# Attention and GEGLU layers on one core: the emitter orders TensorE by a timed event model, with exponentials without a bias operand, a compact out-projection and a two-phase start of layer 2

## The chip, the cores and the metric

The kernel runs on one core of a Trainium2 chip. The metric is device time in microseconds (us) of one execution; lower is better. Every program was run several times, always beside runs of the kernel before on the same chip.

## The reference

Two identical layers, each an attention block and a GEGLU block with residuals. 2048 tokens, width 512, 32 heads of 16, FFN width 1792, all in bfloat16.

```python
def _A_ref(x, wqkv, wo):                       # attention
    q, k, v = split_heads(x @ wqkv)            # 32 heads of 16
    p = softmax((q @ k.T) * 16 ** -0.5)        # 2048 x 2048 for each head
    return merge_heads(p @ v) @ wo

def _B_ref(x, w_gate, w_up, w_down):
    return (gelu_tanh(x @ w_gate) * (x @ w_up)) @ w_down

for _ in range(2):
    x = x + _A_ref(layernorm(x), wqkv, wo)
    x = x + _B_ref(layernorm(x), w_gate, w_up, w_down)
```

## The kernel before

The work of a layer is 32 *units*: 4 blocks of 512 queries times 8 groups of 4 heads. A unit has 64 score tiles (128 keys x 512 queries), made in 22 *slots* of two or three tiles, each slot in one of two sets of three PSUM banks (PSUM is the memory that the matmuls write into). In a slot ScalarE takes the exponential of two or three tiles in one ACTIVATE. In 16 of the 22 slots the third tile goes to VectorE instead, which makes a piecewise approximation of the exponential in int16 (tile `fPI`, then three shifted copies `fPP`). TensorE multiplies all of these with V (17 columns: 16 of V and a column of ones, which gives the row sums) into one accumulator bank. After a query block's 8 units come its out-projection, layer norm and FFN, the *post* of the block, as side work among the units of the next block.

The kernel is written by a small emitter: every operation is appended to its engine's list with the tiles it reads and writes, and semaphores are derived from that. Each engine runs its list in order. So if TensorE's next operation waits, every later one on TensorE waits with it, ready or not. The order comes from counters of steps and "tokens", not from times:

```python
def mm512(pairs, rkeys, evac, cols=512):       # a projection: 4 or 8 matmuls into bank 6
    b = misc.next()
    ...
    pe(fn, rkeys, [BK[b]])
    evac(b)                                    # VectorE reads the bank, at once in the list
    return 216.0 * n + 100

while nxt < len(seqs) or unit_order:           # one slot for each step
    ...
    if state["gslots"] is not None: emit_gslots()   # 7 gelu slots in a row
    a_slot(layer, u, tiles, ds)                # 3 score matmuls, exponential
    if shifts: do_shift()
    if step % 2 or not posts: run_pv(step)     # weighted sums of slots at least LAG = 2 old
    flush_norm(step)
    tokens = min(CAP, tokens + RATE)
    if step % 2 == 0:
        ...                                    # projections and posts while tokens last
```

A post waits for the normalised tile by counting steps (`yield from delay(12)`), then puts its out-projection into TensorE's list. The exponential has its bias as a column in memory:

```python
sch.op("act", lambda e: e.activation(PT[...], PS[:, b0:b0 + na, :], ACTF.Exp,
                                     bias=EBIAS[:, 0:1], scale=1.0 / (OCT * LOG2E)), ...)
```

The out-projection uses a padded layout: a head group's 16 real rows in each 32, so 8 matmuls of which half the rows are zero. The reciprocals of the row sums go through DRAM and come back into one buffer (`NRB = 1`):

```python
for i, g in enumerate(gs):                     # 4 head groups at a time
    for j in range(4):
        dma("sp", ..., RB[32 * j:32 * j + 16, slot, :], src, ...)
    sch.op("pool", ... AT[:, g, :] = OS[:, os_, :] * RB[:, slot, :])
def out_proj(qb, qt):
    return mm512([(AT[:, g, qt * 128:(qt + 1) * 128], WOP[:, g, :]) for g in range(NG)], ...)  # NG = 8
```

Of the kernel before, what the change touches and what calls it, by code (L numbers as in the profile page):

```python
# [14 lines left out]
AP = bass.AP  # L15
# [5 lines left out]
class _Op:  # L21
    __slots__ = ("eng", "idx", "fn", "deps", "waits", "sig", "val", "grp", "vc", "marks")

    def __init__(self, eng, idx, fn, grp=None):
        self.eng = eng
        self.idx = idx
        self.fn = fn
        self.deps = {}
        self.waits = []
        self.sig = False  # L30
        self.val = 0
        self.grp = grp
        self.vc = None
        self.marks = ()


class _Sched:
    SELF_ORDERED = ("pe",)

    def __init__(self):  # L40
        self.streams = {}
        self.track = {}
        self.last_w = {}
        self.last_r = {}
        self.order = []
        self.groups = {}
        self.alias = {}

# [13 lines left out]
    def add_engine(self, name):  # L62
        self.streams[name] = []
        self.track[name] = []

# [4 lines left out]
    def op(self, eng, fn, r=(), w=(), grp=None):  # L70
# [35 lines left out]
        self.order.append(o)  # L106
        return o
# [46 lines left out]
def _emit_fast(nc, es, x_in, wqkv, wo, wg, wu, wd, out, n_rep=2):  # L154
# [22 lines left out]
    NPH = 4  # L177
    OCT = 1024.0
    LOG2E = 1.4426950408889634
    QSCALE = OCT * LOG2E * DH ** -0.5  # L180
    SHIFT = 3.0
    LOG2_4M = 2.0566325
    L_LO, L_HI = 32.0, 1e30
# [13 lines left out]
    WOP = sb("fWOP", [128, NG, D], BF)  # L197
    NWR = 5
# [5 lines left out]
    EBIAS = sb("fEBIAS", [128, 1], F32)  # L204
# [4 lines left out]
    NPS = 4  # L209
    PP = sb("fPP", [128, NPS, 2048], I16)  # L210
    NQS = 4
    Q = sb("fQ", [128, NQS, 512], BF)
    NOS = HB + 2
    OS = sb("fOS", [128, NOS, 512], F32)
    LT = sb("fLT", [128, 128], F32)
    NRB = 1
    RB = sb("fRB", [128, NRB, 512], F32)
    AT = sb("fAT", [128, NG, 512], BF)
# [23 lines left out]
    class Ring:  # L242
        def __init__(self, banks):
            self.banks = list(banks)
            self.pos = 0

        def next(self):
            self.pos += 1
            return self.banks[self.pos % len(self.banks)]

    misc = Ring([MISC])

    def dma(eng, grp, dst, src, r=(), w=(), serial=False):
        if grp not in sch.groups:
            sch.add_dma_group(grp, serial=serial)
        sch.op(eng, lambda e: e.dma_start(dst, src), r=r, w=w, grp=grp)  # L256

    def pe(fn, r, w):
        sch.op("pe", fn, r=r, w=w)
# [3 lines left out]
    for t in range(4):  # L263
        dma("pool", "ldx0_%d" % t, X[:, t, :], x_in[0, 128 * t:128 * (t + 1), :], w=[("X", t)])
    for b in range(1, NQB):
        dma("pool", "ldx%d" % b, X[:, 4 * b:4 * b + 4, :],
            x_in[0, 512 * b:512 * (b + 1), :].rearrange("(a p) c -> p a c", p=128),
            w=[("X", 4 * b + i) for i in range(4)])
    dma("sp", "ldw_k", WK[:], wq_src[:, :, D:2 * D], w=[("WK",)])
    dma("sp", "ldw_q", WQ[:], wq_src[:, :, 0:D], w=[("WQ",)])  # L270
    dma("sp", "ldw_v", WV[:], wq_src[:, :, 2 * D:3 * D], w=[("WV",)])
# [7 lines left out]
    for j in range(4):  # L279
# [3 lines left out]
    sch.op("pool", lambda e: e.memset(EBIAS[:], -SHIFT / LOG2E), w=[("EBIAS",)])  # L283
    sch.op("dve", lambda e: e.memset(PS[:, ACC, :], 0.0), w=[BK[ACC]])
    sch.op("pool", lambda e: e.memzero(WOP[:].rearrange("p a b -> p (a b)")),
           w=[("WOP", j, p) for j in range(4) for p in range(2)])
    for j in range(4):
        for p in range(2):
            src = AP(wo.tensor, wo.offset + (32 * j + 16 * p) * D, [[D, 16], [128 * D, NCK], [1, D]])
            dst = AP(WOP, 32 * j * NG * D + p * D, [[NG * D, 16], [2 * D, NCK], [1, D]])  # L290
            dma("sp", "ldw_o%d%d" % (j, p), dst, src, w=[("WOP", j, p)])
    sch.op("pool", lambda e: e.memset(AP(VP, 16, [[NKT * H * VW, 128], [VW, NKT * H]]), 1.0), w=[("VPONE",)])
    sch.op("pool", lambda e: e.memset(RB[:], 0.0), w=[("RB", i, j) for i in range(NRB) for j in range(4)])
    sch.op("pool", lambda e: e.memset(OKL[:], 1.0), w=[("OKL",)])
    sch.op("pool", lambda e: e.memset(OKV[:], 1.0), w=[("OKV",)])
    sch.op("pool", lambda e: e.memset(LT[:], 1.0), w=[("LT", i, j) for i in range(HB) for j in range(4)])
# [13 lines left out]
    def wload():  # L310
# [12 lines left out]
        dma("sp", "wr%d" % s, dst, src, w=[("WR", s)], serial=True)  # L323
# [11 lines left out]

    def xn(i, alt):
        return AT[:, i, :] if alt else HT[:, i, :]

    def xnkey(i, alt):
        return ("AT", i) if alt else ("HT", i)  # L340

    def ln_tiles(tts, check=False, alt=False):
        n = len(tts)
        for i, tt in enumerate(tts):
            sch.op("dve", lambda e, i=i, tt=tt: e.bn_stats(ST[:, i, :], X[:, tt, :]), r=[("X", tt)], w=[("ST", i)])  # L345
            sch.op("dve", lambda e, i=i: e.bn_aggr(MV[:, i, :], ST[:, i, :]), r=[("ST", i)], w=[("MV", i)])
# [3 lines left out]
        sch.op("pool", lambda e: e.tensor_scalar(LNS[:, 0, 0:n], var, LN_EPS, None, op0=ALU.add), r=mvk, w=[("LNS",)])  # L350
        sch.op("pool", lambda e: e.tensor_tensor(LNS[:, 1, 0:n], LNS[:, 0, 0:n], CM05[:, 0:n], op=ALU.pow),
               r=[("LNS",), ("CM05",)], w=[("LNS",)])
        sch.op("pool", lambda e: e.tensor_scalar(LNS[:, 2, 0:n], mean, -1.0, None, op0=ALU.mult),
               r=mvk + [("LNS",)], w=[("LNS",)])
        for i, tt in enumerate(tts):
            sch.op("pool", lambda e, i=i, tt=tt: e.tensor_scalar(  # L356
                xn(i, alt)[:, 0:D], X[:, tt, :], LNS[:, 2, i:i + 1], LNS[:, 1, i:i + 1], op0=ALU.add, op1=ALU.mult),
                r=[("X", tt), ("LNS",)], w=[xnkey(i, alt)])
        if check:
            sch.op("dve", lambda e: e.scalar_tensor_tensor(OKV[:, 0:n], var, L_HI, OKV[:, 0:n],  # L360
                                                           op0=ALU.is_le, op1=ALU.mult),
                   r=mvk + [("OKV",)], w=[("OKV",)])

    def transpose_tile(i, tt, alt=False, eng="dve"):
        b = misc.next()

        def fn(e):
            for ck in range(NCK):
                ins = e.transpose(bankbf(b)[:, ck * 128:(ck + 1) * 128], xn(i, alt)[:, ck * 128:(ck + 1) * 128],
                                  IDN[:, :])  # L370
            return ins

        pe(fn, [xnkey(i, alt), ("IDN",)], [BK[b]])
        dst = XNT[:, :, tt * 128:(tt + 1) * 128]
        src = bankbf(b)[:, 0:NCK * 128].rearrange("p (a b) -> p a b", a=NCK)
        if eng == "act":
            sch.op("act", lambda e: e.activation(dst, src, ACTF.Copy), r=[BK[b]], w=[("XNT", tt)])
        else:
            sch.op("dve", lambda e: e.tensor_copy(dst, src), r=[BK[b]], w=[("XNT", tt)])
        return 56.0 * NCK + 100  # L380

    def mm512(pairs, rkeys, evac, cols=512):
        b = misc.next()
        n = len(pairs)

        def fn(e):
            for i, (l, r_) in enumerate(pairs):
                ins = e.matmul(bank(b)[:, 0:cols], lhsT=l, rhs=r_, start=(i == 0), stop=(i == n - 1))  # L388
            return ins

        pe(fn, rkeys, [BK[b]])
        evac(b)
        return 216.0 * n + 100
# [4 lines left out]
    def qproj(layer, qb, c):  # L398

        def evac(b):  # L400
            for p in range(2):
                slot = (layer * NU + qb * NG + 2 * c + p) % NQS
                sch.op("dve", lambda e, p=p, slot=slot: e.tensor_scalar(Q[:, slot, :], bank(b), QMASK[:, p:p + 1], None,
                                                                       op0=ALU.mult),
                       r=[BK[b], ("QMASK",)], w=[("Q", slot)])
        return mm512([(WQ[:, ck, 128 * c:128 * (c + 1)], XNT[:, ck, 512 * qb:512 * (qb + 1)]) for ck in range(NCK)],
                     xk(qb) + [("WQ",)], evac)

    def kproj(c, kb):
        return mm512([(WK[:, ck, 128 * c:128 * (c + 1)], XNT[:, ck, 512 * kb:512 * (kb + 1)]) for ck in range(NCK)],  # L410
                     xk(kb) + [("WK",)],
                     lambda b: sch.op("dve", lambda e: e.tensor_copy(KT[:, c, 512 * kb:512 * (kb + 1)], bank(b)),
                                      r=[BK[b]], w=[("KT", c, kb)]))
# [4 lines left out]
    def vproj(c, kb):  # L418
        b = misc.next()

        def fn(e):
            for t in range(4):
                for ck in range(NCK):
                    tt = 4 * kb + t
                    ins = e.matmul(bank(b)[:, 128 * t:128 * (t + 1)], lhsT=XNT[:, ck, tt * 128:(tt + 1) * 128],
# [3 lines left out]
        pe(fn, xk(kb) + [("WV",)], [BK[b]])  # L429
        sch.op("dve", lambda e: e.tensor_copy(  # L430
            VP[:, 4 * kb:4 * kb + 4, 8 * c:8 * c + 8, 0:16],
            bank(b).rearrange("p (t h d) -> p t h d", t=4, h=8)),
            r=[BK[b]], w=[("VP", c, kb)])
        for m in range(NM):
            kbs = sorted({(3 * m + o) // 4 for o in D_KT})
            if kbs[-1] != kb:
                continue
            for r in range(4):
                for ph in range(1, NPH):
# [1344 lines left out]
```

## Time and profile before

| | before |
|---|---|
| median time | 2260.03 us (2259.66 to 2261.19) |
| ScalarE, TensorE, VectorE busy | 74%, 77%, 65% |
| mean granted TensorE clock | 0.876 |
| back-to-back start to start of an exponential, 128x1024 / 128x1536 | 0.997 / 1.424 us |
| first / longest ScalarE gap at the layer boundary | 28.9 / 48.7 us |

First the head of the profile page of the kernel before: busy time by engine, then the span in 40 equal slices. A digit is the busy share of a slice in tenths; PEclk is the TensorE clock that the chip granted, in tenths of full speed.

```profile
PE 1739.5 (77%) x13889; PEld 506.4 (22%) x13889; DVE 1461.2 (65%) x2413; ACT 1660.8 (74%) x1484; POOL 341.2 (15%) x587
...
PE   4888869677886868868679887796868877686847
...
ACT  2789968688796877868318898686978879686941
...
PEclk8998889887998779988789888898879988898969
```

ScalarE (ACT) falls from 9 to 6 or 7 again and again, and to 3 and 1 in slices 20 and 21, the boundary of the two layers. A steady limit would look flat.

Next the groups of instructions by shape: operation, count, busy us, mean ns of one, idle time before them and its releaser. L724 is the exponential, L676 the gelu.

```profile
L724 ACT ACTIVATE fPT<-fPS,fEBIAS 128x1024 bf16<-128x1024 f32 x1152 | 1214.3, 1127 | 304.3 <-PE fPS L719 299.6
L724 ACT ACTIVATE fPT<-fPS,fEBIAS 128x1536 bf16<-128x1536 f32 x256 | 376.0, 1545 | 141.3 <-PE fPS L719 138.9
L676 ACT ACTIVATE fHT<-fPS 128x1024 bf16<-128x1024 f32 x56 | 57.4, 1024 | 110.6 <-PE fPS L670 110.5
```

The gelu of the same shape has no bias operand and takes 1024 ns. Durations overlap: the trace's starts of exponentials that follow each other without a gap are 997 ns apart, not 1127.

Then the waits: engine, tile and line, what ended the wait, total us, times, longest us.

```profile
ACT fPT L724 <- PE fPS L719: 438.4, 349, 48.7
...
PE fPS L613 <- DMA fWR<-in_B_w_down_dram: 93.2, 24, 13.7
PE fPS L388 <- POOL fAT L523: 90.7, 8, 26.4
...
PEld fPS L613 <- DMA fWR<-in_B_w_down_dram: 30.6, 35, 2.1
```

PE is TensorE's multiplication, PEld its weight load. They stood 93 us and 31 us behind w_down, and PE 91 us behind GpSimd's normalised tile (26 us of it in the tail). While TensorE stood there, no score tiles came, and ScalarE waited too. Two pieces of the timeline show one of each, and a third the layer boundary:

```profile
285.55 7.62 ACT L724 ACTIVATE fPT<-fPS,fEBIAS 128x1024 bf16<-128x1024 f32 x7 [0.24 <-PE fPS L719]
305.21 1.54 ACT L724 ACTIVATE fPT<-fPS,fEBIAS 128x1536 bf16<-128x1536 f32 x1 [12.04 <-PE fPS L719]
```

```profile
439.64 1.86 PE L613 MATMUL fPS<-fWR,fHT 128*128 128x512 bf16 x4 [12.74 <-DMA fWR<-in_B_w_down_dram]
```

```profile
1122.97 1.02 ACT L676 ACTIVATE fHT<-fPS 128x1024 bf16<-128x1024 f32 x1 [28.89 <-PE fPS L670]
...
1184.39 1.54 ACT L724 ACTIVATE fPT<-fPS,fEBIAS 128x1536 bf16<-128x1536 f32 x1 [48.73 <-PE fPS L719]
```

### The profile page before, as it was taken

What the parts mean: (1) busy time and instruction counts of PE and PEld (TensorE: products, weight loads), DVE (VectorE), ACT (ScalarE), POOL (GpSimd) and SP (SyncE); (2) the same over time, 40 slices, a digit from 0 to 9 for tenths busy, and PEclk for the clock granted to TensorE, in tenths of its full rate; (3) what the DMA queues carried; (4) which work ended last, traced back from release to release, by engine and by line L of the source; (5) the groups of instructions that cost most, each with busy time, mean ns of one, the idle gap of its engine ahead of it and who ended that gap; (6) DMA issues with size and microseconds to landing.
All of it is one profiled execution on the core that took longest, in us unless ns stands there. A gap on an engine that the chain in (4) does not pass through costs nothing.

```text
span 2259.5 us, 34638 instructions
## 1 busy us (share of the span) xinstructions
PE 1739.5 (77%) x13889; PEld 506.4 (22%) x13889; DVE 1461.2 (65%) x2413; ACT 1660.8 (74%) x1484; POOL 341.2 (15%) x587
## 2 busy tenths in 40 slices
PE   4888869677886868868679887796868877686847
PEld 1331113121221112212223211221112211131113
DVE  5787766676486756857438777475756857666733
ACT  2789968688796877868318898686978879686941
POOL 6560020000101001013106400100001000200000
PEclk8998889887998779988789888898879988898969
DMA  5000002310123001230150000024001230023102
GB/s 135 1 2 11 2 10 62 113 29 10 32 71 107 1 11 48 70 91 1 30 176 1 7 6 9 22 67 129 4 11 48 74 96 1 16 60 109 44 15 85
DMA packets 132725, 102.74 MB, mean 45 GB/s; under 512 B 10960, under 2 KB 126416, under 8 KB 132560
## 3 DMA queue, kind: packets, MB, share of 16 engines
q1 hardware_dynamic: 130400, 96.25, 15.0%
q0 software_dynamic: 2160, 4.19, 0.7%
q8 instruction: 115, 1.88, 0.3%
q14 instruction: 50, 0.41, 0.1%
HBM read 95.16 MB, written 2.62 MB: 43 GB/s over the span
## 4 chain that ended last, share of the span: by engine, by line
DVE 31%; PE 29%; ACT 22%; DMA 7%; POOL 4%; SPq 4%; issue 2%; DVEq 0%; POOLq 0%
ACT fPT L724 21%; DVE fPI L737 13%; DVE fPP L755 9%; PE fPS L808 7%; PE fPS L388 7%; PE fPS L719 7%; PE fPS L670 4%; DMA fRB<-rscr 4%; SPq L256 4%; POOL fAT L523 3%; PE fPS L613 2%; DVE fHT L600 2%; DMA fWR<-in_B_w_down_dram 2%; DVE fST L345 1%; DVE fOS L535 1%
## 5 line engine op out<-in xcount | busy, mean ns | idle before, releaser
L724 ACT ACTIVATE fPT<-fPS,fEBIAS 128x1024 bf16<-128x1024 f32 (+1 forms) x1408 | 1580.6, 1203 | 445.6 <-PE fPS L719 438.4
L737 DVE TENSOR_SCALAR fPI<-fPS 128x512 int16<-128x512 f32 x1024 | 690.3, 682 | 384.5 <-PE fPS L719 383.0
L719 PE MATMUL fPS<-fQ,fKT 32*128 32x512 bf16 x4096 | 597.6, 422 | 193.7 <-ACT fPT L724 98.2
L808 PE MATMUL fPS<-fPT,fVP 128*17 128x512 bf16 x3072 | 550.6, 416 | 27.9 <-DVE fOS L535 9.4
L755 DVE TENSOR_SCALAR fPP<-fPI 128x2048 int16<-128x2048 int16 x768 | 526.5, 697 | 8.8
L808 PE MATMUL fPS<-fPP,fVD 128*17 128x512 f16 x3072 | 473.1, 407 | 10.9 <-DVE fPP L755 10.8
L808 PE MATMUL fPS<-fPI,fVP 128*17 128x512 f16 x1024 | 400.2, 423 | 18.3 <-DVE fPP L755 8.7
L719 PEld LDWEIGHTS fPS<-fQ,fKT 32*128 32x128 bf16 x4096 | 143.7, 92 | 797.7 <-ACT fPT L724 527.1
L523 POOL TENSOR_TENSOR fAT<-fOS,fRB 128x512 bf16<-128x512 f32 x64 | 85.0, 1328 | 1420.5 <-DMA fRB<-rscr 1314.0
L613 PE MATMUL fPS<-fWR,fHT 128*128 128x512 bf16 x448 | 128.4, 402 | 94.8 <-DMA fWR<-in_B_w_down_dram 93.2
L442 POOL TENSOR_SCALAR fVD<-fVP 128x34 f16<-128x34 f16 x384 | 152.3, 399 | 107.6 <-DVE fVP L430 78.6
L808 PEld LDWEIGHTS fPS<-fPT,fVP 128*17 128x17 f16 x3072 | 112.4, 88 | 228.9 <-issue 99.0
L388 PE MATMUL fPS<-fWOP,fAT 128*128 128x512 bf16 x256 | 74.3, 447 | 90.7 <-POOL fAT L523 90.7
L676 ACT ACTIVATE fHT<-fPS 128x1024 bf16<-128x1024 f32 x56 | 57.4, 1024 | 110.6 <-PE fPS L670 110.5
L808 PEld LDWEIGHTS fPS<-fPP,fVD 128*17 128x17 f16 x3072 | 107.2, 91 | 83.9 <-DVE fPP L755 32.2
L388 PE MATMUL fPS<-fXNT,fWR 128*128 128x512 bf16 x448 | 111.8, 381 | 13.1 <-DVE fHT L600 12.9
L555 DVE TENSOR_TENSOR fX<-fPS,fX 128x512 f32<-128x512 f32 x32 | 22.1, 692 | 147.0 <-PE fPS L388 146.6
L600 DVE TENSOR_TENSOR fHT<-fPS,fHT 128x512 bf16<-128x512 f32 x112 | 76.8, 686 | 54.7 <-PE fPS L388 54.6
L670 PE MATMUL fPS<-fXNT,fWR 128*128 128x512 bf16 x448 | 101.6, 389 | 4.4 <-ACT fPT L724 3.7
L808 PEld LDWEIGHTS fPS<-fPI,fVP 128*17 128x17 f16 x1024 | 77.9, 89 | 94.7 <-issue 44.4
L613 PEld LDWEIGHTS fPS<-fWR,fHT 128*128 128x128 bf16 x448 | 33.4, 99 | 158.2 <-issue 107.4
L356 POOL TENSOR_SCALAR fHT<-fX,fLNS 128x512 bf16<-128x512 f32 x56 | 61.8, 1119 | 1.5
(58 smaller groups left out, 653.1 us busy)
## 6 DMA issues: line engine op xcount, KB each, us to landing
fWR<-in_B_w_down_dram SPq DMA_DIRECT2D x203, 256.0 KB, 2.9
fWR<-in_B_w_gate_dram SPq DMA_DIRECT2D x56, 256.0 KB, 3.3
fWR<-in_B_w_up_dram SPq DMA_DIRECT2D x56, 256.0 KB, 2.8
fRB<-rscr SPq DMA_DIRECT2D x256, 32.0 KB, 1.8
fLT<-fOS SPq DMA_DIRECT2D x256, 2.0 KB
fX<-in_A_x_dram POOLq DMA_DIRECT2D x3, 1024.0 KB, 11.8
out_dram<-fXNT SPq DMA_DIRECT2D x16, 128.0 KB, 2.5
fX<-in_A_x_dram POOLq DMA_DIRECT2D x4, 256.0 KB, 7.3
```

Of the source, the lines that this page charges most:

```text
L256: sch.op(eng, lambda e: e.dma_start(dst, src), r=r, w=w, grp=grp)
L388: ins = e.matmul(bank(b)[:, 0:cols], lhsT=l, rhs=r_, start=(i == 0), stop=(i == n - 1))
L442: sch.op("pool", lambda e, dst=dst, src=src, ph=ph: e.tensor_scalar(dst, src, 2.0 ** (-ph / NPH), None, op0=ALU.mult), r=[("VP", c, k) for ...
L523: sch.op("pool", lambda e, g=g, slot=slot, os_=os_: e.tensor_tensor(AT[:, g, :], OS[:, os_, :], RB[:, slot, :], op=ALU.mult), r=[("OS", os ...
L600: lambda b, ft=ft: sch.op("dve", lambda e: e.tensor_tensor(HT[:, ft, :], bank(b), HT[:, ft, :], op=ALU.mult), r=[BK[b], ("HT", ft)], w=[(" ...
L613: ins = e.matmul(bank(b)[:, 0:D], lhsT=HT[:, ft, i * 128:(i + 1) * 128], rhs=WR[:, s, jj * D:(jj + 1) * D], start=(ft == 0), stop=(ft == N ...
L670: ins = e.matmul(bank(b0 + jj), lhsT=wchunk(s, jj, ck), rhs=XNT[:, ck, xs], start=(ck == 0), stop=(ck == NCK - 1))
L719: ins = e.matmul(bank(b0 + k), lhsT=KT[32 * j:32 * j + 32, c, kt * 128:(kt + 1) * 128], rhs=Q[32 * j:32 * j + 32, qs, :], start=True, stop ...
L724: sch.op("act", lambda e: e.activation(PT[:, p, 0:512 * na].rearrange("p (a b) -> p a b", a=na), PS[:, b0:b0 + na, :], ACTF.Exp, bias=EBIA ...
L737: sch.op("dve", lambda e: e.tensor_scalar(PI[:, gi, 512 * r:512 * (r + 1)], bank(b0 + n - 1), DBIAS, 0.0, op0=ALU.add, op1=ALU.max), r=[bk ...
L755: sch.op("dve", lambda e: e.tensor_scalar(PP[:, s, :], PI[:, gi, :], int(OCT) * ph // NPH, None, op0=ALU.add), r=[("PI", gi, r) for r in r ...
L808: ins = e.matmul(PS[32 * j:32 * j + VW, ACC, :], lhsT=l, rhs=r_, start=a, stop=z, tile_position=(0, 32 * j), skip_group_check=True)
```

## The change

One idea and several companions.

1. *Order by modelled time.* Every operation gets a modelled cost and latency; the emitter keeps a clock for each engine. At each point it asks which of TensorE's candidates is ready now: the next score slot first, then weighted sums, then side work. A piece of side work goes in only if its inputs are ready and it fits before the moment at which the next score slot can start. VectorE's jobs are chosen in the same way.
2. *No bias operand.* The shift of the exponential goes, so ScalarE's instruction has immediates alone.
3. *Compact out-projection.* Odd head groups are moved by a DMA into the free rows, so the out-projection has 4 matmuls for each tile and not 8.
4. *Two phases.* The first six units of layer 2 do 16 of their 22 slots on the keys of the first three query blocks (phase A), before the fourth block has left layer 1, and the rest later (phase B).
5. *Smaller things.* A sixth weight buffer and a second buffer for reciprocals, fewer and larger scalings of V on GpSimd, three `fPP` buffers and not four, more buffers for Q and for evacuated sums, no VectorE exponentials at the start, and a group of them goes to ScalarE when the model says that VectorE is over 3 us late. Also, from the third unit on, slots without a VectorE tile are dealt among those with one and no longer stand at the unit's end (in phases A and B they stay apart).

The core of the diff, with cuts:

```diff
+    def ready(self, eng, r=(), w=()):          # modelled time at which all operands are there
+        t = 0.0
+        for k in r: ... t = max(t, self.track[p[0]][p[1]].seen)
+        for k in w: ...
+        return t
-    def op(self, eng, fn, r=(), w=(), grp=None):
+    def op(self, eng, fn, r=(), w=(), grp=None, cost=0.1, lat=0.15, at=0.0):
+        start = max(self.free[eng], at, self.ready(eng, r, w))
 ...
+        self.free[eng] = start + cost
+        o.seen = start + cost + lat
 ...
-        sch.op(eng, lambda e: e.dma_start(dst, src), r=r, w=w, grp=grp)
+        return sch.op(eng, lambda e: e.dma_start(dst, src), r=r, w=w, grp=grp, cost=0.45, lat=lat)
 ...
-    while nxt < len(seqs) or unit_order:       # steps and tokens
+    while True:
+        t = now[0] = max(now[0], sch.free["pe"])
+        pump(t)                                # VectorE's jobs up to now
 ...
+        F = fill_ready()
+        if F is not None and F <= t + 0.02:
+            fill()                             # the next score or gelu slot
+            continue
+        limit = 99.0
 ...
+        if F is not None:
+            limit = max(F, sch.free["act"] - 0.44) - t
+        its = pv_ready(t)
 ...
+        if fit >= 1 and (full >= want or full and (rest or press)):
+            pv(its, min(fit, full, 6))         # weighted sums
+            continue
+        for src in sources:                    # layer 1 head, projections, post
+            p = src.peek()
 ...
+            if bs is None or piece_ready(p, bs) > t + 0.02 or p.cost > limit + src.tol():
+                continue
 ...
-                                             PS[:, b0:b0 + na, :], ACTF.Exp, bias=EBIAS[:, 0:1], scale=...),
+                                                 PS[:, b0:b0 + na, :], ACTF.Exp, scale=...),
 ...
+        if layer and NQB > 1:
+            for part, pat in (("A", pattern[:4 * NM]), ("B", pattern[4 * NM:])):
+                for u in us[:NPART]:           # NPART = 6
+                    seqs += [(layer, u, part, tl, ds, k == len(pat) - 1) for k, (tl, ds) in enumerate(pat)]
+            us = us[NPART:]
 ...
+                dst = ATS[:, c % 2, :] if odd else AT[:, c, :]
+                pool(... dst = OS[:, os_, :] * RB[:, slot, :] ...)
+                if odd:
+                    for j in range(4):
+                        dma("sp", ..., AT[32 * j + 16:32 * j + 32, c, :], ATS[32 * j:32 * j + 16, c % 2, :], ...)
```

## The prediction

> **What bounds the kernel now.** No engine is full: the page gives ScalarE 74%, TensorE 77% (modelled ends, an upper figure), VectorE 65% of 2259.5 us. Grouping ScalarE's 1408 exponentials by head group (22 each, 64 units, from the timeline), the quietest units start 24.7 us apart; 64 of them are 1581 us. The other ~680 us is stalls: units 0, 2 and 4 of each later query block take 41-43 us. Waits and timeline name them: about 12 us at each out-projection (behind GpSimd's normalised tile), about 14 us in each down-projection (TensorE waits for w_down: 93+31 us in all), gelu bursts at 1.7 us per slot against 1.02 us of gelu, with two 1.28 us table loads, gaps of 28.9 and 48.7 us at the layer boundary, about 57 us lost in the first 81 us, and a tail of about 90 us after the last exponential.
>
> **What changes, costed.**
> 1. ScalarE: the bias operand goes. The trace has 1114 ns for 128x1024 with it and 1024 ns for gelu of that shape without. The Trainium skill ("ScalarE: Activation LUTs", What ACT_TABLE_LOAD costs) states about 93 ns per pointer operand; the trace's 90 ns agrees. Back-to-back starts are now 0.99 and 1.42 us, part overlapped already; I estimate 50-70 ns x 1408 = 70-100 us off, on the critical path where ScalarE is fed.
> 2. TensorE order: side work goes in only when its inputs are modelled ready and it fits before the next score fill. The 12 and 14 us stalls of six in-loop blocks (about 155 us) should mostly go, with 20-50 us of small gaps.
> 3. Layer boundary: six units of layer 2 do 16 of 22 slots on the first three query blocks, about 90 us of ScalarE work over a 97 us chain: 70-80 us back, less six extra evacuations (0.7 us VectorE).
> 4. Out-projection: 256 -> 128 matmuls; the last four tiles took 9.3 us, so 4.6 us at the tail. The second RB buffer shortens the four-step 4.5 us chain; moving odd heads costs another DMA (about 1.8 us). Tail: about 10 us better; gelu 14.6, up 12.1, down 10.8 us stay.
> 5. Head: 384 GpSimd scalings of V become 96 larger ones, initialisation is deferred: 15-30 us.
> 6. Against: the first two units use no VectorE exponentials (+0.43 us x 32); late VectorE hands tiles to ScalarE (estimate 0-50 us).
>
> **Sum.** 2260 - 85 - 155 - 35 - 75 - 10 - 20 + 30 = 1910 at worst; from below, 64 units at 23.2 us = 1485, bursts 123, head 40, tail 80, other 50 = about 1780. I take **1840 us**, range **1735 to 1950**. Chances: faster by over 2% 0.95, within 2% 0.03, slower 0.02.
>
> **What would show it.** Exponentials near 1.02 and 1.45 us (1). ScalarE 80-87% of the span. Inside the loop no TensorE wait over 3 us for GpSimd's tile or w_down (2). Largest ScalarE gap at the boundary under 12 us (3). 128 out-projection matmuls (4). Tail still 75-90 us. Fewer than 1024 VectorE exponential tiles; mean clock at or above 0.876.
>
> **What would make it wrong.** The emitter assumes full-clock matmuls; the windows view grants 0.74-0.88 in pure attention. If pieces run longer than modelled, each delays a fill and ScalarE stays at 75% (1950+). VectorE at about 80% may free PSUM banks late. SyncE's queue is in order: weight loads may stand behind the new DMAs. If model and chip agree and a denser TensorE holds the clock at 1.0, 1740 is possible.

## The result, and the profile after

The kernel after takes 1830.13 us (median of 4 runs, 1824.53 to 1835.9) against 2259.85 us: a ratio of 0.81, 95% interval 0.8073 to 0.8128. Ratios here and below are the mean time of one kernel's runs over that of the other's of the same rounds, so not quite the ratio of the medians that are quoted. Outputs are correct.

The head of the page after:

```profile
PE 1570.5 (86%) x13401; PEld 465.0 (25%) x13401; DVE 1365.1 (75%) x2225; ACT 1558.5 (85%) x1484; POOL 228.3 (12%) x281
...
PE   5888889988898989999789788899989998898828
...
ACT  3699998999989999999579489989998999989911
...
PEclk9987979989899979999989858898989988999969
```

ScalarE is now at 9 nearly everywhere except at head and tail and around slices 20 to 24, the boundary. Its groups (L944 exponential, L904 gelu):

```profile
L944 ACT ACTIVATE fPT<-fPS 128x1024 bf16<-128x1024 f32 x1032 | 998.7, 1054 | 64.8 <-PE fPS L939 60.2
L944 ACT ACTIVATE fPT<-fPS 128x1536 bf16<-128x1536 f32 x376 | 537.4, 1477 | 76.1 <-PE fPS L939 75.3
L904 ACT ACTIVATE fHT<-fPS 128x1024 bf16<-128x1024 f32 x56 | 57.4, 1025 | 81.6 <-PE fPS L898 81.4
```

The waits that answer to those of before:

```profile
ACT fPT L944 <- PE fPS L939: 135.6, 142, 23.7
...
PE fPS L484 <- DMA fAT<-fATS: 27.3, 1, 27.3
...
PEld fPS L740 <- DMA fWR<-in_B_w_down_dram: 6.5, 12, 1.4
...
PE fPS L740 <- DMA fWR<-in_B_w_down_dram: 2.8, 5, 1.4
```

ScalarE's waits for scores fell from 438 us to 136 us. The 91 us of TensorE behind the normalised tile are one wait of 27 us, at the very end of the program, where there is nothing else to do. The waits for w_down fell from 93 and 31 us to 2.8 and 6.5 us (overlap counted once: from 111 to 7.9 us). The boundary, where the longest ScalarE gap remains:

```profile
988.73 18.52 ACT L944 ACTIVATE fPT<-fPS 128x1536 bf16<-128x1536 f32 x16 [0.16 <-PE fPS L939]
1030.94 14.52 ACT L944 ACTIVATE fPT<-fPS 128x1536 bf16<-128x1536 f32 x12 [23.69 <-PE fPS L939]
```

Where the time came from is best read by stage. I cut each trace at the start of every 22nd exponential, which counts ScalarE's progress in units (in layer 2 the first 132 slots are six units' worth, whatever their order). Us:

| stage | before | after | difference |
|---|---|---|---|
| start to the second unit | 81.2 | 74.9 | -6.3 |
| units 1 to 7 | 189.8 | 168.5 | -21.3 |
| units 8 to 31 | 801.6 | 614.9 | -186.7 |
| first six units' worth of layer 2 (boundary) | 262.0 | 219.9 | -42.1 |
| rest of layer 2 | 835.0 | 661.6 | -173.4 |
| after the last exponential (tail) | 89.9 | 86.7 | -3.2 |
| span | 2259.5 | 1826.4 | -433.1 |

So 360 of 433 us come from these two interior stages, not from head, boundary or tail. The ten quietest units fell from 25.1 to 22.0 us on average. What did not change is a block's gelu burst: from the last exponential ahead of it to the first behind it 13.7 us in the old trace (six blocks; at the boundary it is part of a hole of 91.6 us) and 14.1 to 14.5 us in the new one (seven blocks).

### The profile page after: what moved, and what is told of

It is laid out like the page before. It is cut to its first block, busy times and chain, and to the rows that moved or that the text cites. A ratio compares the mean times of both kernels' runs of the same rounds, so it can differ in the third digit from the quotient of the medians.

```text
span 1826.4 us, 33054 instructions
## 1 busy us (share of the span) xinstructions
PE 1570.5 (86%) x13401; PEld 465.0 (25%) x13401; DVE 1365.1 (75%) x2225; ACT 1558.5 (85%) x1484; POOL 228.3 (12%) x281
## 4 chain that ended last, share of the span: by engine, by line
PE 41%; ACT 35%; DVE 16%; POOL 3%; DMA 2%; issue 1%; SPq 1%; DVEq 0%; POOLq 0%
ACT fPT L944 34%; PE fPS L1046 12%; PE fPS L939 11%; PE fPS L484 7%; DVE fPI L978 6%; PE fPS L898 6%; DVE fPP L999 5%; PE fPS L740 4%; POOL fVD L539 2%; DVE fQ L503 1%; SPq L268 1%; DVE fOS L656 1%; PE fPS L524 1%; DVE fST L430 1%; DMA fWR<-in_B_w_down_dram 0%
## 5 line engine op out<-in xcount | busy, mean ns | idle before, releaser
L944 ACT ACTIVATE fPT<-fPS 128x1024 bf16<-128x1024 f32 (+1 forms) x1408 | 1478.5, 1167 | 140.9 <-PE fPS L939 135.6
L978 DVE TENSOR_SCALAR fPI<-fPS 128x512 int16<-128x512 f32 x904 | 606.5, 686 | 197.6 <-PE fPS L939 194.0
L1046 PE MATMUL fPS<-fPT,fVP 128*17 128x512 bf16 x3192 | 496.4, 417 | 14.0 <-DVE fPP L999 9.4
L999 DVE TENSOR_SCALAR fPP<-fPI 128x2048 int16<-128x2048 int16 x678 | 465.4, 717 | 35.6 <-PE fPS L1046 31.4
L1046 PE MATMUL fPS<-fPP,fVD 128*17 128x512 f16 x2712 | 421.2, 416 | 11.3 <-DVE fPP L999 7.7
L1046 PE MATMUL fPS<-fPI,fVP 128*17 128x512 f16 x904 | 280.1, 415 | 0.4 <-DVE fPP L999 0.4
L635 POOL TENSOR_TENSOR fAT<-fOS,fRB 128x512 bf16<-128x512 f32 x32 | 42.5, 1328 | 1032.4 <-DMA fRB<-rscr 1032.4
L904 ACT ACTIVATE fHT<-fPS 128x1024 bf16<-128x1024 f32 x56 | 57.4, 1025 | 81.6 <-PE fPS L898 81.4
L539 POOL TENSOR_SCALAR fVD<-fVP 128x136 f16<-128x136 f16 x96 | 58.9, 615 | 37.7 <-DVE fVP L546 30.2
L437 POOL TENSOR_SCALAR fLNS<-fMV 128x4 f32<-128x4 f32 x16 | 3.7, 229 | 457.0 <-DVE fMV L431 456.9
L503 DVE TENSOR_SCALAR fQ<-fPS,fQMASK 128x512 bf16<-128x512 f32 x64 | 44.9, 744 | 20.1 <-PE fPS L484 20.1
L484 PE MATMUL fPS<-fWO,fAT 128*128 128x512 bf16 x128 | 34.4, 397 | 29.0 <-DMA fAT<-fATS 27.3
```

The source lines that it names most:

```text
L484: ins = e.matmul(bank(bs[0])[:, 0:cols], lhsT=l, rhs=r_, start=(i == 0), stop=(i == n - 1))
L503: ops.append((lambda e, p=p, slot=slot: e.tensor_scalar(Q[:, slot, :], bank(b), QMASK[:, p:p + 1], None, op0=ALU.mult), [BK[b], ("QMASK",) ...
L539: pool(lambda e, dst=dst, src=src, ph=ph: e.tensor_scalar(dst, src, 2.0 ** (-ph / NPH), None, op0=ALU.mult), [("VP", c, k) for k in range( ...
L904: sch.op("act", lambda e: e.activation(HT[:, 2 * k:2 * k + 2, :], PS[:, b0:b0 + 2, :], ACTF.Gelu_apprx_tanh), r=bks, w=[("HT", 2 * k), ("H ...
L944: o = sch.op("act", lambda e: e.activation(PT[:, p, 0:512 * na].rearrange("p (a b) -> p a b", a=na), PS[:, b0:b0 + na, :], ACTF.Exp, scale ...
L978: dve(0, [(lambda e: e.tensor_scalar(PI[:, gi, 512 * r:512 * (r + 1)], bank(b0 + n - 1), DBIAS, 0.0, op0=ALU.add, op1=ALU.max), [bks[-1]], ...
```

## The experiments

Theory 1 was that of the prediction: ScalarE paces the kernel wherever it is fed, and the change feeds it (an order that knows when operands are ready and what fits) and shortens its instruction. The main rival was that TensorE is the pace-maker, being 86% busy on the page; then the ScalarE instruction would not matter, and the gain would come from a denser TensorE and its clock. Each part has a smaller rival of its own. Unless it is said otherwise, an edit is of the kernel after, with 3 rounds, and is compared through ratios to the kernel before; the kernel after is 0.8100. All twelve gave correct results.

### before_nobias: only the bias operand, in the kernel before

```diff
-    SHIFT = 3.0
+    SHIFT = 0.0
-    L_LO, L_HI = 32.0, 1e30
+    L_LO, L_HI = 64.0, 1e30
-    ... ACTF.Exp, bias=EBIAS[:, 0:1], scale=1.0 / (OCT * LOG2E))
+    ... ACTF.Exp, scale=1.0 / (OCT * LOG2E))
```

> The old kernel with only the bias operand of the exponential taken away (shift 0 instead of 3, limit of the row sums 64 instead of 32). Theory 1 (ScalarE sets the pace of the units between the stalls): back-to-back starts fall from 0.997/1.424 us to 0.905/1.331 us, quiet units from 24.7 to about 22.7 us, and the time falls by 60 to 130 us, to 2130-2200 us; less than the full 1408 x 93 ns = 131 us, because units that stall on TensorE absorb a part. Rival (TensorE order and its clock set the pace everywhere): less than 15 us, 2245 us or more.

Measured: 2226.17 us (2216.32 to 2229.46), ratio 0.9855 (0.9831 to 0.9879): 34 us less than the 2260.03 us of before by the medians, 33 us by the ratio, between both expectations. Starts fell to 0.920 (median; shortest 0.903) and 1.330 us, as expected, but a quiet unit only from 24.5 to 24.2 us (the shortest of each). The waits view of this run shows where the rest went:

```profile
ACT fPT L724 <- PE fPS L719: 510.4, 496, 48.6
```

Before it was 438.4 us in 349 waits. So 147 new waits took 72 us of what the shorter instruction had given. In the old order even the quiet units stood close to a second limit, TensorE's fixed list as I read it, only 1 to 2% below ScalarE's. Theory 1 was too simple for the old kernel: ScalarE was the nearest limit there, not the only one.

### after_bias: the bias operand given back, order untouched

```diff
+    EBIAS = sb("fEBIAS", [128, 1], F32)            # zeros
-    ... ACTF.Exp, scale=1.0 / (OCT * LOG2E)), r=bks[:na], ...
+    ... ACTF.Exp, bias=EBIAS[:, 0:1], scale=1.0 / (OCT * LOG2E)), r=bks[:na] + [("EBIAS",)], ...
```

> The new kernel with a 128x1 column of zeros given back as the bias operand; the emitter is not told, so the order of every engine stays what it is. Theory 1 (the new kernel is paced by ScalarE nearly everywhere): starts back at 0.997/1.424 us, and 1408 x 93 ns = 131 us less what falls into waits: 1930-1960 us. Rival (TensorE, 86% busy on the page, is the pace-maker now): 1830-1855 us.

Measured: 1916.59 us (1914.39 to 1921.57), ratio 0.8494 (0.8479 to 0.8509): 87 us slower than the kernel after by the medians, far above the rival's range but short of the 1930 us that I had expected at least. Starts went back to 0.996 and 1.423 us. The ScalarE wait for scores in this run:

```profile
ACT fPT L946 <- PE fPS L941: 104.0, 89, 22.3
```

It fell from 135.6 us, so a part of the 131 us (1408 x 93 ns) was taken up by waits, and 87 us was not. TensorE as the only pace-maker, the rival, is refuted: the same TensorE list with the same work ran 87 us longer because ScalarE's instruction was 93 ns longer. The mean granted clock was lower too (0.888 against 0.908); what it added to the 87 us is not separated. The same edit was worth 33 us in the old order and 87 us in the new one.

### after_bias_told: the same, with the model told

```diff
 (after_bias, and)
-    ... cost=0.072 + 0.4267 * na ...
+    ... cost=0.165 + 0.4267 * na ...
```

> As after_bias (1917 us, ratio 0.849), but the event model is told the 93 ns. If a 9% error in the modelled length of a ScalarE operation already spoils the order, this is 10 us or more faster than after_bias: ratio under 0.845. Rival (the order is not that delicate, semaphores keep it right and slack hides the rest): within 8 us, 0.846-0.853.

Measured: 1929.22 us (1924.69 to 1937.19), ratio 0.8542 (0.8513 to 0.8571). It is not faster, rather 0.6% slower (the intervals just miss each other); the expected 0.846 to 0.853 of the rival was missed by a hair on the other side. An error of 9% in one modelled cost did not spoil the order. Why knowing better made it no better is left open; told, the emitter left 940 tiles to VectorE instead of 904, so it was another order in other ways too.

### after_nofit: readiness without fitting

```diff
         limit = 99.0
+        fits = 99.0
         ...
-            limit = max(F, sch.free["act"] - 0.44) - t
+            fits = max(F, sch.free["act"] - 0.44) - t     # not used: limit stays 99
```

> The new kernel with the test of fitting switched off: side work and weighted sums still wait until the model says that their inputs are there, but they may now overrun the moment at which the next score fill could start. Theory 1 (fitting is what keeps ScalarE fed): ScalarE waits for scores grow from 136 us by 40 us or more, 1870-1910 us. Rival (readiness is what mattered; the two score slots hide an overrun of up to about 1 us): within 15 us of 1830.

Measured: 1852.88 us (1846.67 to 1855.4), ratio 0.8205 (0.8188 to 0.8222): 24 us (1.3%) slower, between the two expectations, nearer to the rival. Fitting matters, but it is the small part. ScalarE's wait for scores grew only from 135.6 to 143.8 us:

```profile
ACT fPT L944 <- PE fPS L939: 143.8, 167, 23.1
```

The other part of the loss is work: 24 more tiles went from VectorE to ScalarE (880 against 904 VectorE tiles, 24 x 0.427 = 10 us of ScalarE; a tile costs it 1.331 - 0.905 us). The two together, 18 us, are the difference of the two traced executions (1844.8 and 1826.4 us).

### after_dmablind: a model that believes transfers to be instant

```diff
-    return sch.op(eng, lambda e: e.dma_start(dst, src), r=r, w=w, grp=grp, cost=0.45, lat=lat)
+    return sch.op(eng, lambda e: e.dma_start(dst, src), r=r, w=w, grp=grp, cost=0.0, lat=0.0)
```

> The new kernel whose event model believes every transfer to be instant (issue and landing cost 0), all else as it is. Theory 1 (knowing when operands are ready is what removed the 12 and 14 us stalls of the old kernel): TensorE again stands behind w_down and behind the normalised tile, ScalarE gaps of 3 us or more return inside the loop, +40 to +150 us, 1870-1980 us. Rival (the sixth weight buffer and the second RB buffer removed those stalls, the order hardly matters): within 15 us of 1830.

Measured: 2047.58 us (2045.21 to 2052.38), ratio 0.9037 (0.9022 to 0.9052): 212 us slower by the ratios, more than the 40 to 150 us expected. The buffers are those of the kernel after, and so are the operations but for 4 tiles (900 VectorE tiles against 904); what differs is the order. Stalls of the old kinds are back:

```profile
ACT fPT L944 <- PE fPS L939: 350.8, 174, 32.1
...
PE fPS L484 <- DMA fAT<-fATS: 133.5, 8, 27.5
...
PEld fPS L740 <- DMA fWR<-in_B_w_down_dram: 80.9, 29, 13.2
PE fPS L740 <- DMA fWR<-in_B_w_down_dram: 66.8, 13, 12.9
```

```profile
277.27 1.49 PE L484 MATMUL fPS<-fWO,fAT 128*128 128x512 bf16 x3 [16.27 <-DMA fAT<-fATS]
278.69 0.61 PE L939 MATMUL fPS<-fQ,fKT 32*128 32x512 bf16 x3
...
279.35 2.10 ACT L944 ACTIVATE fPT<-fPS 128x1024 bf16<-128x1024 f32 x2 [17.29 <-PE fPS L939]
```

The out-projection sits in the list too early, waits 16 us for the moved heads, and the score slot behind it comes 17 us late to ScalarE. The old kernel did not move heads and stood 7 to 10 us at this place, so the 212 us are the price of this order in the new kernel, not what the old one lost. The w_down waits, up to 13 us, are of the old size. By stage, units 8 to 31 take 720.1 us (614.9 with the true model), the rest of layer 2 775.8 us (661.6); head, boundary and tail do not move. The rival, that the added buffers by themselves removed these stalls, is refuted: the buffers are in this kernel too. Whether the order would do without them was not tried.

### after_onephase: no two phases

```diff
-    NPART = 6
+    NPART = 0
-        cl = range(min(NCK, NPART // 2)) if layer else [0]
+        cl = [0]
```

> The new kernel without the two phases: the second layer's units run whole, one after the other. Theory 1: the chain of the last block of layer 1 stands open again, about 90 us of ScalarE work no longer laid over it, against about 48 us of gaps that stayed with the phases: 1865-1910 us. Rival (the event-ordered emitter alone closes the boundary, by running the last block's side work early): under 15 us, below 1845 us.

Measured: 1869.73 us (1861.16 to 1879.22), ratio 0.8284 (0.8253 to 0.8316): 41 us slower, inside the expectation. The hole of the old kernel is back:

```profile
928.11 1.02 ACT L904 ACTIVATE fHT<-fPS 128x1024 bf16<-128x1024 f32 x1 [61.53 <-PE fPS L898]
...
987.35 2.37 ACT L944 ACTIVATE fPT<-fPS 128x1536 bf16<-128x1536 f32 x2 [46.01 <-PE fPS L939]
```

The boundary stage takes 263.2 us, as in the kernel before (262.0), against 219.9: the two phases are the whole gain there, and the rest of the change by itself gained nothing at the boundary. The hole, from the last exponential before to the first after, is even longer than the old one (122.1 against 91.6 us); faster units made up for it. The edit also changed the sharing of work: 92 VectorE tiles in this stage against 60 with two phases, so the phases gave ScalarE 32 tiles, 14 us at 0.427 us each.

### after_alwaysd: VectorE keeps its groups

```diff
-    DVE_LATE = 3.0
+    DVE_LATE = 1e9
```

> The new kernel that never hands a VectorE group back because VectorE is late (only a busy buffer or the first two units still do). Theory 1 (VectorE near its limit: handing 120 tiles to ScalarE, 120 x 0.427 = 51 us, avoids longer stalls): about 980-1010 VectorE tiles and 5 to 50 us slower, 1835-1880. Rival (the hand-over only costs ScalarE time): 20 to 40 us faster, 1790-1810.

Measured: 1814.33 us (1808.29 to 1820.84), ratio 0.8009 (0.7982 to 0.8035): 20 us (1.1%) faster by the ratios, 16 us by the medians, close to the rival's 20 to 40 us. Theory 1 fell here: the rule of handing groups back costs ScalarE time and buys nothing. 956 tiles stayed on VectorE (I had expected 980 to 1010; some groups still fail on a busy buffer), that is 52 more than 904, or 22 us of ScalarE at 0.427 us each, which is what came off. VectorE is then 78% busy.

### after_vd_dve and after_vd_tail: the boundary and the tail

In the trace of the kernel after, 48 scalings of V for layer 2 stand on GpSimd from 886.3 to 921.3 us, right ahead of the last block's layer norm. The first edit moves them to VectorE; the second also changes the last normalisation.

```diff
-    pool(<VD = V * 2**(-ph/4)>, ..., 0.5)
+    (layer 2)  vds.append((<the same>, ..., 0.22)) ; dve(1, vds, got((layer, "vd", c)))
 (after_vd_tail, and in the last normalisation only)
-    for i, g in enumerate(gs):  load RB(i); multiply(i); move odd head(i)      # all issued by SyncE
+    load RB(0), RB(1); multiply 0, 1; load RB(2), RB(3); move 1; multiply 2, 3; move 3
+    # the four issues of each alternate between SyncE and ScalarE
```

> The new kernel with the scaled copies of V for layer 2 made on VectorE (48 operations at about 0.2-0.25 us each) instead of GpSimd, where they stood 35 us (48 x 0.73 us) ahead of the last block's layer norm. Theory 1 (the 24 us ScalarE gap and the 8, 12 and 4 us ones at the boundary are GpSimd's queue): the layer norm moves up by about 28 us, the gaps over 3 us at the boundary fall from 48 to under 25 us: 1795-1812 us. Rival (the last block's own matmuls and w_down transfers bound the boundary): within 8 us of 1830.

> As after_vd_dve, and in the last normalisation the second pair of reciprocal loads goes out before the move of the first odd head, with the issues dealt over SyncE and ScalarE. If SyncE's in-order queue makes the 27 us from the last evacuation to the out-projection: 6 to 10 us less of tail (86.7 us after the last exponential to 77-81), 6 to 10 us below after_vd_dve. Rival (latencies of transfers, not their issue): under 3 us.

after_vd_dve: 1833.7 us (1830.22 to 1836.35), ratio 0.81 (0.8087 to 0.8114): no gain; Theory 1 fell. The operations themselves were cheap, as expected:

```profile
L540 DVE TENSOR_SCALAR fVD<-fVP 128x136 f16<-128x136 f16 x48 | 10.0, 208 | 1.6
```

The 12 and 4 us gaps are gone, but one gap before phase B grew:

```profile
1031.58 18.68 ACT L952 ACTIVATE fPT<-fPS 128x1536 bf16<-128x1536 f32 x15 [36.80 <-PE fPS L947]
```

The boundary stage is 220.7 us against 219.9. The out-projection of the last block now ended at 926.7 us instead of 904.6 us, spread among score slots and projections: GpSimd's queue was one gate, TensorE's priorities another behind it.

after_vd_tail: 1829.43 us (1825.84 to 1832.35), ratio 0.8082 (0.8068 to 0.8095). Its trace has a tail of 79.9 us against 87.3 in after_vd_dve; the ratio moved by only 0.0018, 4 us, with overlapping intervals. So the issue order is worth 7 us in this trace, and 4 us by the times, not surely more than nothing. The shorter tail itself is not chance: in the four traces that have this edit (this one and the three below) it is 78.5 to 80.3 us, in the eight other traces of the new order 86.1 to 88.0 us.

### best_late_tail, best_post_tail, best_all: towards a better kernel

```diff
 best_late_tail:   DVE_LATE = 1e9, and the tail of after_vd_tail
 best_post_tail:   best_late_tail, and
-        for src in sources:
+        for src in ([sources[0], sources[2], sources[1]] if pace["haste"] else sources):
                                        # last block of a layer: its post before K and V projections
 best_all:         best_post_tail, and V's scaling for layer 2 on VectorE
```

> The new kernel without the hand-over of late VectorE groups (measured alone: 1814 us, ratio 0.801) and with the dealt-out tail issue (measured on top of another edit: 0.8082 against 0.8100, about 4 us). If the two add: ratio about 0.799, about 1806-1812 us. Rival (their ends meet): no better than 0.801.

> As best_late_tail, and in the last block of each layer the block's own work (out-projection, FFN) is asked before the K and V projections of the next layer. If the late out-projection of that block (spread over 10 us with GpSimd's scaling, over 30 us without) is a matter of priority, it finishes within about 6 us, gelu starts earlier than 932 us on the trace, and 5 to 15 us come off: ratio 0.793-0.797. Rival (the layer norm behind GpSimd's 35 us of scaling of V sets gelu's start in any case): within 4 us of best_late_tail.

> As best_post_tail, with the scaling of V for layer 2 on VectorE. after_vd_dve took GpSimd out of the way and gained nothing, since the out-projection then ended 22 us later behind fills and projections. If GpSimd's queue and TensorE's priority are two gates in a row, opening both gains what neither does alone: gelu of the last block starts 20 us or more earlier than 938 us, ScalarE's largest boundary gap falls under 20 us, ratio 0.785-0.793 (1775-1795 us). Rival (matmuls and w_down transfers of the last block bound it): within 5 us of best_post_tail.

best_late_tail: 1808.84 us (1806.12 to 1813.97), ratio 0.7999 (0.7982 to 0.8017), as expected. best_post_tail: 1804.91 us (1800.8 to 1808.61), ratio 0.7988 (0.7967 to 0.8009). best_all: 1816.48 us (1815.98 to 1818.44), ratio 0.8037 (0.8023 to 0.805).

best_post_tail is clearly faster than both kernels (1.4% below the kernel after), but against best_late_tail its difference is inside the intervals and short of the ratio of 0.793 to 0.797 expected, although gelu of the last block did start earlier (918.9 us against 933.2). best_all was expected to be the best and is the worst of the three: gelu started at 917.7 us and the gap before phase B fell to 12.6 us, but a new gap of 31.6 us came earlier, and its boundary stage is the longest of all (225.3 us). best_post_tail has that earlier gap too (31.0 us before 895.8), and its timeline shows GpSimd just before it:

```profile
869.43 1.27 POOL L641 TENSOR_TENSOR fAT<-fOS,fRB 128x512 bf16<-128x512 f32 x1 [82.00 <-DMA fRB<-rscr]
...
878.56 1.26 POOL L641 TENSOR_TENSOR fAT<-fOS,fRB 128x512 bf16<-128x512 f32 x1 [5.98 <-DMA fRB<-rscr]
...
881.95 0.23 POOL L437 TENSOR_SCALAR fLNS<-fMV 128x4 f32<-128x4 f32 x1
```

The layer norm of the third block (L437) starts directly behind four multiplies that wait for transfers of the fourth. That the norm could have run earlier, and that this costs the gap, I argue from the order and did not test.

## Why the prediction was right

The time, 1830 us, lies 10 us from the predicted 1840 and inside the range. The mechanism held in the main: ScalarE is the nearest limit of the new kernel (after_bias), TensorE blocked by early side work costs most when it returns (after_dmablind), and the check list came true in all points but one. Exponentials took 1.031 and 1.457 us (medians; 1.02 and 1.45 predicted), ScalarE is at 85% (80 to 87), VectorE tiles 904 (fewer than 1024), out-projection matmuls 128, tail 86.7 us (75 to 90), mean clock 0.908 (at or above 0.876). The miss is the largest boundary gap: 23.7 us, not under 12.

That the total came within 10 us is partly luck. The terms as summed gave 1910 us, the count from below 1780, and 1840 was a choice between them; the terms took off 350 us where 430 came off, and single ones erred in both directions:

| term | predicted | measured | by |
|---|---|---|---|
| 1. bias operand | 70 to 100 us | 87 us | after_bias |
| 2. blocked TensorE | about 155 us, and 20 to 50 of small gaps | 212 us for knowing transfers, 24 us for fitting | after_dmablind, after_nofit |
| 3. two phases | 70 to 80 us | 41 us | after_onephase |
| 4. tail | about 10 us | 3.2 us | stages |
| 5. head | 15 to 30 us, less part of term 6 | 6.3 us to the second unit | stages |
| 6. against | 14 us, and 0 to 50 of handed-over tiles | one unit without VectorE tiles and not two, 7 us (0.43 x 16); hand-over costs about 20 us | kernel and trace, after_alwaysd |

Each single removal is measured against the full change, so the terms need not add up to 430 us. What the other companions gave (the new dealing of slots within a unit, the added buffers) was not measured.

- *Term 1* came out right in total by two errors. I took 50 to 70 ns for each instruction because I thought that the overlap of consecutive ACTIVATEs had already swallowed a part. The full 92 to 93 ns (0.997 to 0.905 us, 1.424 to 1.331 us) came off; of 131 us in all, 44 fell into time in which ScalarE had waited anyway. The Trainium skill ("ScalarE: Activation LUTs", What ACT_TABLE_LOAD costs) states that each pointer operand adds about 93 ns; the runs agree within a nanosecond, and show that it holds for back-to-back starts as well. I had not foreseen that the gain depends so much on the order: 33 us in the old kernel, 87 in the new one. In the old kernel I called quiet units ScalarE-bound, and they were bound at nearly the same length by TensorE's list.
- *Term 2* was probably too small, as far as a removal from the new kernel can tell. I counted the two large stalls of six blocks. The old trace also had 170 us in ScalarE gaps of 0.5 to 3 us, of which 69 us are left.
- *Term 3* was too large. I set 90 us of work against a 97 us chain as if one could lie over the other entirely. Phase A competes for TensorE, GpSimd and VectorE with the very chain it is to cover: the last block's gelu began at 938.5 us with two phases and at 928.1 us without, although its normalisation had begun earlier with them (872.8 us against 875.7). The stage still takes 220 us for 132 us of quiet units (6 x 22.0) and a 14 us gelu burst.
- *Term 4*: the out-projection did halve on the chain, as the tail shows. Lines are start us, length us, and what; first the kernel before, then the kernel after.

```profile
2193.26 1.76 DMA fRB<-rscr
2195.09 0.09 issue
2195.18 1.27 POOL fAT L523
2196.50 9.22 PE fPS L388 x32
```

```profile
1760.25 2.00 DMA fRB<-rscr
1762.33 0.09 issue
1762.42 1.27 POOL fATS L635
1763.71 0.51 SPq L268
...
1765.53 1.80 DMA fAT<-fATS
1767.33 0.14 issue
1767.46 4.48 PE fPS L484 x12
```

From the last evacuation (2170.1 and 1740.2 us) to the out-projection it took 26.4 us before and 27.2 us after: moving the odd heads and issuing those moves ate what the second RB buffer gave.
- *The feared clock*: the model assumes full-clock matmuls, and the chip granted 0.59 to 1.00 in the 50 us windows of the kernel after. The time stayed inside the range all the same: slot starts are ordered by semaphores, and a 9% wrong ScalarE cost moved the time by less than 1%; a model blind to transfers moved it by 12%. But the record does not clear the clock. The four executions of the kernel after took 1824.5, 1828.3, 1832.0 and 1835.9 us at mean clocks of 0.912, 0.908, 0.901 and 0.894. In its trace the eleven interior units without gelu whose mean clock was below 0.8 took 25.7 us on average with 2.1 us of ScalarE waits, the 27 above 0.95 took 22.9 us with 0.4 us (interior: units 2 to 31 and 39 to 62, counted from 0). Whether the lower clock made them wait, or the waiting lowered the clock, no run here separates. The Trainium skill ("TensorE: Matmul & The Clock Gate", Part 1) says that the activity gate knows only half and full clock; the clock record of both traces agrees, it holds 0.5 and 1.0 alone, so the window means are mixtures.

What bounds the boundary stage stays open. Five variants of it (after, after_vd_dve, best_late_tail, best_post_tail, best_all) lie between 216 and 225 us; where one gap shrank, another grew. The shortest is in a run that was not aimed at it: after_bias_told needs 207.8 us, although its exponentials start 91 to 92 ns later one after the other (0.996 and 1.423 us). So another order (there with 72 VectorE tiles in the stage against 60) can gain 12 us more here; what gave them was not looked for.

## What to carry to other kernels

An engine that runs its list in order passes one early operation's wait on to everything behind it, so put side work into a list when its operands will be there, above all those that come by DMA; here taking that knowledge away cost 212 us, nine times as much as no longer fitting side work between the slots (24 us). A shorter instruction on the nearest engine pays fully only when no other engine's order holds the same pace: test it in both orders before crediting it. When idle time is filled with other work, count what that work takes from the chain it is meant to hide; here about half of the hidden 90 us came back.

## What the Trainium skill lacked or had wrong

- "ScalarE: Activation LUTs", What ACT_TABLE_LOAD costs: it adds a drain of about 1380 ns to the 1283 ns load. In both traces the load follows 17 to 19 ns after the last ACTIVATE and takes 1283 ns, and the next ACTIVATE starts 11 or 12 ns later in 12 of 15 loads of each kernel: about 1.31 us for a switch, with no separate drain.
- The same section: consecutive ACTIVATEs overlap by about 93 ns. Here, by medians, they overlap by 126 ns without a bias operand (1.031 us long, 0.905 us apart) and by 118 to 142 ns with it (before, after_bias), so 128x1024 costs 0.905 us in a row where the page's figures give about 0.946 (186 + 853 - 93 ns, an estimate from the page).
- "Trainium Kernel Development and Optimization", Key Constraints: issuing from several engines saves only the sequencer's issue time. The trace of after_vd_tail fits that (tail 87.3 to 79.9 us, with reordering and dealing out together, so the share of the dealing is not shown), but the page gives no size; on SyncE one issue took 0.42 us (RB load), 0.57 us (row sums) and 0.59 us (move of an odd head) here, by medians.
